# Output copies ahead of other VectorE work at block seams, a changed prologue order and two moved units, in a fused Fourier filter and SwiGLU kernel

## Chip, cores, metric

One core of one Trainium2 chip. The time is the device time of one execution, in microseconds (us), as a median over runs. The **span** in a profile is the time from the first to the last instruction of one profiled execution; it is some 2 us shorter than the run's time (890.6 in a run of 892.44 us). Every run lists its mean granted TensorE clock, where 1.0 is full speed.

## The reference

```python
X = np.fft.rfft(x, axis=1)                       # x: 8 sequences, 3008 tokens, 256 channels
y = np.fft.irfft(X * (filt_r + 1j * filt_i)[None], n=3008, axis=1)
x = y.reshape(24064, 256)
xn = x / np.sqrt(np.mean(x * x, axis=-1, keepdims=True) + 1e-6) * rms_g
g, val = xn @ w_gate, xn @ w_val                 # d_ff = 1536
out = (g * (1 / (1 + np.exp(-g))) * val) @ w_out
```

## The kernel before

The transforms are matmuls in two stages. "Stage A" transforms a sequence along one factor of its length. "Stage B" transforms along the other: a *unit* is a pair of matmuls into a bank (`psb`), followed by two products with the filter tables `fr` and `fi` and then by inverse matmuls. The feed-forward part runs over blocks of 512 tokens; each block takes 12 *slots* (one per 128 columns of d_ff, `JT = 12`). In a slot TensorE makes gate and value (`pg`, `pv`), ScalarE makes `sg`, VectorE multiplies them to `hh`, and two slots later `down` adds `hh` times `w_out` to the output banks `po0` and `po1`. Units of the *next* sequence are spread over the slots of the current one; only sequence 0 has nothing to hide behind, so it has a *prologue* of some 47 us, in which dummy matmuls (`warm_up`) keep TensorE active.

VectorE takes its work in the order of issue, so the loop that issues the slots sets the order:

```python
def at(slot, fn, *a):
    todo = {q_unit: late, swap_unit: pre}.get(fn, plan).setdefault(slot, [])
    ...
for i in range(len(items) + 4):
    for fn, a in pre.get(i, ()):      # half-swaps of summed units
        fn(*a)
    if i < len(items):
        gv(*items[i])                 # pg, pv, sg, hh
    for fn, a in plan.get(i, ()):     # stage A and B units, inverses, loads
        fn(*a)
    if 2 <= i < len(items) + 2:
        down(*items[i - 2])           # after a block's last slot: copies po0 (ScalarE), po1 (VectorE)
    for fn, a in late.get(i, ()):
        fn(*a)
```

A stage B unit of a later sequence, and the two ways in which VectorE can be spared (`summed`: one full product, two half-swaps, GpSimd adds; `eng = gpsimd`: ScalarE copies the bank, GpSimd makes both products):

```python
def b_unit(b, i, ps=None):
    ps = b_mm(b, i)                                   # bank "mb", one buffer, for b > 0
    f1, f2 = filt(2 * i, 2)
    ... # cut: the tiles s1 and s2
    if b and summed(b, i):
        nc.vector.tensor_tensor(out=s1, in0=ps, in1=f1, op=ALU.mult)      # L252
        return                                        # half-swaps L278, L276 follow in swap_unit
    eng = nc.vector
    if (i in (3, 5, 8, 12)) if b else (i in (3, 7, 9, 12)):
        eng = nc.gpsimd
        ... # cut: the tile v
        nc.scalar.activation(out=v, in_=ps, func=AXT.Copy)                # L266
        ps = v
    eng.tensor_tensor(out=s1, in0=ps, in1=f1, op=ALU.mult)                # L268
    eng.tensor_tensor(out=s2, in0=ps, in1=f2, op=ALU.mult)                # L269
```

The middle of the prologue, where ScalarE (`A`) copies filter tables to the other half of the partitions (`f_dup`), and `inverses` of the second unit of a pair ends with ScalarE's copy of the pair's banks to `gT` (L578; `pgt` is the bank):

```python
products(1); stage_b(5); t1_copy(5, 1)
... # cut
products(4, 7)                       # 7, 9 and 12 go to GpSimd
... # cut
products(5); inverses(3); stage_b(9); products(6, 9); stage_b(10, 11)
inverses(4); products(8); stage_b(12); inverses(5)
f_dup(3, 1, A, 0, 4)
products(12); ...; products(10); stage_b(13, 14); inverses(6)
f_dup(3, 1, A, 4, 8)
inverses(7); products(11); stage_b(15); inverses(8); products(13)
```

## Time and profile before

893.53 us, median of 3 runs (893.45 to 894.48).

| | before | how to read it |
|---|---|---|
| span of the profiled run | 890.6 us, clock 0.999 | undisturbed |
| first gate matmul (`pg<-xn`) starts | 47.15 us | end of the prologue |
| from there to the end | 843.4 us | 588 slots |
| busy share of TensorE, VectorE, ScalarE, GpSimd | 98, 77, 70, 49% | "busy" of TensorE includes the drain |

A matmul's bar in a timeline is longer than its share of the engine, so I use the distances between starts: what a start comes later than the normal distance (0.109 us after a 128x256 matmul, 0.216 after a 128x512, the median of its form after a smaller one) is a **hole**. Over the 843.4 us the holes of more than 0.03 us are 22 and sum to 8.4 us.

### The profile page before, as it was taken

The numbers are of one execution on the slowest core, as the hardware profiler recorded it, in microseconds if no ns is written. First come the engines' busy times: TensorE is split into PE (matmuls) and PEld (weight loads), VectorE is DVE, ScalarE is ACT, GpSimd is POOL, SyncE is SP. The second block draws the span as 40 slices with busy tenths as digits, with TensorE's granted clock in tenths as the row PEclk, the third lists the DMA queues.
The fourth block names the chain that finished last, engine by engine and source line by source line (L and its number), as shares of the span: only waits on it lengthen the run. The fifth ranks groups of instructions, "written<-read, shape, count | busy, mean of one in ns | idle before, by whom it ended". The sixth has DMA issues, their size and how long they took to land.

```text
span 890.6 us, 17468 instructions
## 1 busy us (share of the span) xinstructions
PE 873.5 (98%) x6258; PEld 559.4 (63%) x6258; DVE 681.5 (77%) x1091; ACT 625.1 (70%) x1068; POOL 435.6 (49%) x392
## 2 busy tenths in 40 slices
PE   8799999999999999999999999999999999999997
PEld 5666666666666666666666666666666666666556
DVE  7866787889987877888688787888878887555555
ACT  7877657677677766877677766787657765676444
POOL 7843830656427661677236662376515762155300
PEclk9999999999999999999999999999999999999999
DMA  8696726675663456335645247233352232222202
GB/s 196 122 196 156 157 67 207 143 158 110 162 159 89 101 111 185 107 90 113 159 119 132 86 81 199 80 94 90 88 163 72 67 90 61 85 66 49 72 24 48
DMA packets 80095, 101.44 MB, mean 114 GB/s; under 512 B 8108, under 2 KB 56684, under 8 KB 79560
## 3 DMA queue, kind: packets, MB, share of 16 engines
q1 hardware_dynamic: 69688, 84.23, 34.8%
q0 software_dynamic: 10240, 15.96, 11.4%
q8 instruction: 49, 0.80, 0.4%
q14 instruction: 38, 0.31, 0.1%
q10 hardware_dynamic: 80, 0.13, 0.1%
HBM read 67.67 MB, written 46.78 MB: 129 GB/s over the span
## 4 chain that ended last, share of the span: by engine, by line
PE 87%; issue 4%; DVE 2%; ACT 2%; DMA 2%; POOL 2%; SPq 0%; ACTq 0%; POOLq 0%; DVEq 0%
PE po L462 26%; PE pg L443 25%; PE pv L443 25%; PE psi L291 3%; PE psb L238 3%; PE psn L323 2%; PE psa L203 2%; DMA fr<-in_filt_r_dram 1%; DVE o L469 1%; ACT fr L516 1%; DVE hh L448 1%; DMA rb<-r_tmp 1%; ACT gT L578 1%; PE psq L352 0%; POOL xc L188 0%
## 5 line engine op out<-in xcount | busy, mean ns | idle before, releaser
L448 DVE TENSOR_TENSOR hh<-pv,sg 128x512 f16<-128x512 f32 (+2 forms) x588 | 392.9, 670 | 190.2 <-ACT sg L447 77.6
L447 ACT ACTIVATE sg<-pg 128x512 f16<-128x512 f32 (+2 forms) x588 | 340.9, 580 | 227.5 <-PE pg L443 217.8
L462 PE MATMUL po<-wo,hh 128*128 128x256 f16 x2244 | 343.2, 272 | 3.8 <-DVE o L469 3.0
L443 PE MATMUL pv<-xn,wv 128*128 128x512 f16 (+2 forms) x1176 | 339.6, 370 | 0.0
L443 PE MATMUL pg<-xn,wg 128*128 128x512 f16 (+2 forms) x1176 | 339.5, 370 | 0.0
L462 PEld LDWEIGHTS <-hh 128*128 128x128 f16 x2256 | 216.4, 98 | 99.0 <-issue 5.3
L282 POOL TENSOR_TENSOR s<-s,s 128x512 f16<-128x512 f16 x102 | 117.9, 1157 | 237.5 <-DVE s L276 165.6
L443 PEld LDWEIGHTS <-wv 128*128 128x128 f16 x1176 | 114.9, 98 | 128.8 <-issue 0.3
L419 POOL TENSOR_TENSOR xn<-y,rb 128x1024 f16<-128x1024 f32 (+1 forms) x45 | 126.0, 2801 | 44.9 <-DMA rb<-r_tmp 37.7
L443 PEld LDWEIGHTS <-wg 128*128 128x128 f16 x1176 | 111.4, 98 | 13.0 <-issue 0.3
L358 POOL TENSOR_TENSOR rho<-u,mhalf 128x4 f32<-128x4 f32 (+1 forms) x48 | 49.1, 1022 | 63.5 <-DVE u L356 63.1
L276 DVE TENSOR_TENSOR s<-psb,fi 64x512 f16<-64x512 f32 x102 | 69.8, 684 | 3.1
L296 ACT ACTIVATE t<-psi 96x512 f16<-96x512 f32 x112 | 66.4, 593 | 8.1 <-PE psi L291 2.7
L278 DVE SCALAR_TENSOR_TENSOR s<-psb,fi 64x512 f16<-64x512 f32 x102 | 70.7, 693 | 1.4
L252 DVE TENSOR_TENSOR s<-psb,fr 128x512 f16<-128x512 f32 x102 | 69.4, 681 | 0.0
L329 ACT ACTIVATE y<-psn,gsb 128x512 f32<-128x512 f32 (+1 forms) x94 | 63.8, 679 | 7.8 <-PE psn L323 0.5
L343 POOL TENSOR_TENSOR sq<-sq 128x512 f16<-128x512 f16 (+1 forms) x35 | 39.6, 1133 | 35.9 <-ACT sq L335 35.9
L335 ACT ACTIVATE sq<-psn 128x512 f16<-128x512 f32 (+1 forms) x94 | 54.8, 583 | 0.0
L208 ACT ACTIVATE t<-psa 128x512 f16<-128x512 f32 x70 | 41.8, 597 | 5.6 <-PE psa L203 2.4
L291 PE MATMUL psi<-s,wi 128*128 128x256 f16 x236 | 44.1, 273 | 0.0
L238 PE MATMUL psb<-t,wb 96*128 96x256 f16 x224 | 43.0, 272 | 0.5 <-DVE s L269 0.5
L323 PEld LDWEIGHTS <-t 128*128 128x128 f16 x368 | 28.4, 98 | 20.6 <-issue 0.4
(104 smaller groups left out, 523.1 us busy)
## 6 DMA issues: line engine op xcount, KB each, us to landing
out_dram<-o SPq DMA_DIRECT2D x83, 256.0 KB
xc<-in_x_dram POOLq DMA_DIRECT2D x56, 192.0 KB, 5.8
z_tmp<-t SPq DMA_DIRECT2D x28, 384.0 KB
t<-z_tmp SPq DMA_DIRECT2D x28, 384.0 KB
g_tmp<-t SPq DMA_DIRECT2D x56, 192.0 KB
rb<-r_tmp SPq DMA_DIRECT2D x41, 256.0 KB
t<-g_tmp SPq DMA_DIRECT2D x21, 384.0 KB
t<-g_tmp SPq DMA_DIRECT2D x7, 320.0 KB
```

The costliest lines, as they stand in the source:

```text
L238: nc.tensor.matmul(ps[:, u, :], w[:, k, :], t, start=True, stop=True)
L252: nc.vector.tensor_tensor(out=s1, in0=ps, in1=f1, op=ALU.mult)
L276: nc.vector.tensor_tensor(out=s2[a], in0=ps[e], in1=f2[e], op=ALU.mult)
L278: nc.vector.scalar_tensor_tensor(out=s2[a], in0=ps[e], scalar=-1.0, in1=f2[e], op0=ALU.mult, op1=ALU.mult)
L282: nc.gpsimd.tensor_tensor(out=s, in0=s1, in1=s2, op=ALU.add)
L291: nc.tensor.matmul(ps[:, u, :], wi_at(q, 2 * i + u), ss[q][:, u, :], start=(q == 0), stop=(q == n - 1))
L296: nc.scalar.activation(out=st[b]["t3"][c][:, 2 * r:2 * r + 2, :], in_=ps[0:KR], func=AXT.Copy)
L419: nc.gpsimd.tensor_tensor(out=xv, in0=yv, in1=rv.unsqueeze(1).to_broadcast([P, 2, n, P]), op=ALU.mult)
L443: nc.tensor.matmul(ps[:, 0:w], wt[:, dt_, ts(jt, P)], xn[:, dt_, :], start=(dt_ == 0), stop=(dt_ == 1))
L447: nc.scalar.activation(out=sg[:, 0:w], in_=pg[:, 0:w], func=AXT.Silu)
L448: nc.vector.tensor_tensor(out=hh[:, 0:w], in0=pv[:, 0:w], in1=sg[:, 0:w], op=ALU.mult)
L462: nc.tensor.matmul(po[s4 // per][:, s4 % per, :], hh[:, ts(s4, P)], wo[:, jt, :], start=(jt == 0 and s4 % per == 0), stop=(jt == JT - 1 an ...
```

## The change

The intent is to close isolated holes on TensorE. At a block's seam (slot 1 modulo 12) stage A and B units are issued after the output copies. Two units of sequence 1 are moved (15 to GpSimd, 1 a slot later), one q step of sequence 2 comes a slot later, and the prologue gets fewer dummy matmuls ("fillers"), one table build earlier and two copies on other engines.

```diff
-        return b > 1 or b == 1 and i in (6, 7, 10, 11, 14, 15)
+        return b > 1 or b == 1 and i in (6, 7, 10, 11, 14)
...
-        if (i in (3, 5, 8, 12)) if b else (i in (3, 7, 9, 12)):
+        if (i in (3, 5, 8, 12, 15)) if b else (i in (3, 7, 9, 12)):
...
             if m == 4:
-                warm_up(6, 0)
+                warm_up(5, 0)
...
-            for g in ((4, 5), (6,), (), (), (7,), ())[m]:
+            for g in ((4, 5), (6,), (), (7,), (), ())[m]:
                 wi_group(g)
             if m == 4:
-                warm_up(3, 0)
+                warm_up(1, 0)
...
-            t1_copy(g, g == 1)
+            t1_copy(g, g % 2)
...
+        t1_copy(4, 0)
         f_dup(0, 0, A, 0, 2)
...
-        t1_copy(4, 1)
         f_dup(0, 0, A, 4, 8)
...
-            todo = {q_unit: late, swap_unit: pre}.get(fn, plan).setdefault(slot, [])
+            at_seam = slot % JT == 1 and fn in (a_unit, b_unit)
+            todo = late if at_seam or fn == q_unit else pre if fn == swap_unit else plan
+            todo = todo.setdefault(slot, [])
...
-                r = (4, 8, 12)
+                r = (5 if (b, m) == (2, 1) else 4, 8, 12)
...
-                b_at = [22 + 7 * i // 4 for i in range(16)]
+                b_at = [22 + 7 * i // 4 + (i == 1) for i in range(16)]
```

## The prediction

> **What bounds the kernel now.** I read the page first (busy shares and the slices), then the table of windows, then the list of what TensorE waited for, then the timeline of VectorE and TensorE around each of those waits, and last the chain of waits over the first 50 us.
>
> ```profile
> PE 873.5 (98%) x6258; PEld 559.4 (63%) x6258; DVE 681.5 (77%) x1091; ACT 625.1 (70%) x1068; POOL 435.6 (49%) x392
> ...
> PE   8799999999999999999999999999999999999997
> ...
> 300.00:400.00 100.00, 100.00 (x699) 64.29 (x698) 80.88 (x129) 74.39 (x129) 55.73 (x50) 1.00 0.50 121
> ```
>
> TensorE is the bound, and in the middle it has nothing left to give: in 300 to 400 us it is busy for 100.00 of 100.00 us at full granted clock (1.00). What can be saved is idle time in the first 45 us, or isolated holes after that. The holes are few, and the list of TensorE's waits names most of them:
>
> ```profile
> PE po L462 <- DVE o L469: 3.0, 6, 0.8
> PE psb L238 <- DVE s L269: 0.5, 2, 0.3
> PE psq L352 <- POOL sq L343: 0.5, 1, 0.5
> ```
>
> "Busy" includes the drain of a pipelined matmul, so I size each hole from the distance between starts: a 128x256 matmul normally starts 0.109 us after the one before it, a 128x512 one 0.216 us (medians over this trace). The largest hole, in the timelines of VectorE and then TensorE:
>
> ```profile
> 109.06 0.69 DVE L448 TENSOR_TENSOR hh<-pv,sg 128x512 f16<-128x512 f32 x1 [0.92 <-PE psb L238]
> 109.66 0.68 DVE L268 TENSOR_TENSOR s<-psb,fr 128x512 f16<-128x512 f32 x1
> 110.26 0.68 DVE L269 TENSOR_TENSOR s<-psb,fi 128x512 f16<-128x512 f32 x1
> 110.86 0.68 DVE L469 COPY o<-po 128x512 f32<-128x512 f32 x1
> ...
> 110.40 0.38 PE L462 MATMUL po<-wo,hh 128*128 128x256 f16 x2
> 111.59 0.38 PE L462 MATMUL po<-wo,hh 128*128 128x256 f16 x2 [0.81 <-DVE o L469]
> ```
>
> A token block is 12 slots. The slot after its last one is a seam: the output bank `po1` is finished, VectorE must copy it out, and TensorE wants the bank again one slot later. Two stage B products (L268, L269) stand ahead of the copy. Third `po` matmul: 111.59 - 110.40 - 0.22 = **0.97 us** lost.
>
> **What the Trainium skill says.** "Perfetto Trace Analysis", section Identifying the Most-Contended Engine, says matmul busy share is no measure of headroom, as matmuls are pipelined; this trace agrees: at 98% busy there are holes of up to 0.97 us that the starts show. "TensorE: Matmul & The Clock Gate" gives in its opening table a strict first-in first-out queue for ScalarE, VectorE and GpSimdE. The trace agrees: the copy above was ready with `po` long before 110.86 and still ran third. So order of issue alone can open or close a hole. The same page, section What's actually happening, says the matmul clock halves after about 3.4 us of idleness; that is why dummy matmuls stand in the prologue. The largest TensorE wait in the first 50 us here is 1.2 us and the granted clock stays 1.00 in the windows, so dropping three of them should not cost clock.
>
> **The change part by part.**
>
> *1. Seams.* At a slot that is 1 modulo 12, stage A and B units go behind the output copies. By the slot formulas only five seams hold such a unit or the moved one: slots 13, 25, 37, 49, 61. From sequence 3 on, no unit falls on a seam, so the rest of the run does not move. Holes, from starts as above: slot 13 (70.4 us) 0.77 - 0.60 = 0.17; slot 25 90.31 - 89.33 - 0.22 = 0.76; slot 37 0.97; slot 61 150.87 - 150.19 - 0.22 = 0.46. In each the copy would start right behind `hh`. At slot 37 it would run 109.66 to 110.34, and TensorE wants the bank at 110.62: no wait. The products end when they ended before. Together 2.36 us.
>
> *2. Unit 15 of sequence 1 moves from VectorE to GpSimd.* Its two half-swaps, done at seam 49, are not reordered by part 1 (swaps stay ahead), so it is moved instead.
>
> ```profile
> 129.00 0.69 DVE L278 SCALAR_TENSOR_TENSOR s<-psb,fi 64x512 f16<-64x512 f32 x1
> 129.70 0.68 DVE L276 TENSOR_TENSOR s<-psb,fi 64x512 f16<-64x512 f32 x1
> 130.42 0.69 DVE L448 TENSOR_TENSOR hh<-pv,sg 128x512 f16<-128x512 f32 x1
> 131.03 0.68 DVE L469 COPY o<-po 128x512 f32<-128x512 f32 x1
> ```
>
> The hole there is 131.76 - 130.71 - 0.22 = 0.83 us and goes. The price: the unit is no longer summed before its inverse, so 4 matmuls of 128x256 in place of 2, 2 x 0.109 = 0.22 us on TensorE; ScalarE gets a copy of 0.6 us, GpSimd two products of 1.27 us for one add of 1.16 us. GpSimd is busy 17.5 of 50 us there, and the inverse comes four slots (over 5 us) later. Net gain 0.61 us.
>
> *3. Unit 1 of sequence 1 one slot later.* At 83.7 us the second stage B matmul waits for products of unit 0: 84.37 - 83.92 = 0.45 us, which goes. But unit 1 now sits one slot before unit 2. I place them by adding durations: unit 1's products end near 87.5 us, while unit 2's matmul (same bank) would be ready near 87.35, so about 0.2 us comes back. Net 0.25 us.
>
> *4. A later q step for block 1 of sequence 2.* TensorE waits for GpSimd's fold at 272.7: 273.35 - 272.70 = 0.65 us. One slot (1.3 us) later the fold, done at 273.3, is in time. The broadcast load stays where it was, with 3 slots in place of 4 after the q step; 0.65 us gained.
>
> *5. Prologue.* Three fillers of 0.216 us go: the first transposes of stage 1 start 0.65 us sooner. One copy of 1.02 us leaves ScalarE after the first filter piece and another comes before it. But the filter tables come by DMA, and the same ScalarE copies wait for those: the first may not start before 20.9 us, the second group not before 25.3 (it ran at 25.82). The last piece ends it all:
>
> ```profile
> 30.09 0.57 SPq L518 DMA_DIRECT2D fr<-fr  x1
> ...
> L268 DVEq EVENT_SEMAPHORE  x6: 21/35/2078, 30.5 to 36.1; - x6
> ...
> 34.78 0.69 DVE L268 TENSOR_TENSOR sg<-psb,fr 128x512 f16<-128x512 f32 x1 [0.38 <-PE pgt L570]
> ```
>
> VectorE's sequencer sat 2.08 us (32.56 to 34.64) in a semaphore wait; the trace's semaphore events show that the DMA issued at 30.09 finished at 34.61. The matmul named in the bracket is only the last event by the profile. From 34.78 VectorE runs without a pause to 38.46, the last product. Nothing in the change moves that DMA. ScalarE's chain beside it gains, after its own DMA waits (27.5 and 28.0 us), some 0.13 us. So I give the prologue **0.13 us**, not the 0.65 us or the 1.02 us that its edits suggest.
>
> Sum: 2.36 + 0.61 + 0.25 + 0.65 + 0.13 = 4.0 us. 893.53 - 4.0 = **889.5 us**.
>
> **The rivals.**
>
> *A. The prologue gives all it seems to.* If the DMAs are not the gate (the chain of waits puts most of 21 to 40 us on ScalarE, where I see its copies back to back), the shift of 0.65 us, perhaps up to 0.9, arrives at the end of the prologue. For it: ScalarE's row names no DMA wait after 21 us but was often ready just at a landing. Against it: the 2.08 us wait. It would make 888.7 to 889.0.
>
> *B. The delayed products take the copy's place as the wait.* With the copy first, products end up to 0.7 us later relative to `hh`, and the bank for stage B has a single buffer. If the next unit's matmul meets them, as in part 3, a hole moves instead of closing. At 37 and 61 the next user of the bank is two or more slots off; only slot 25 is tight. It would make 890 to 890.5.
>
> *C. Another engine becomes the bound.* VectorE at 40.3 of 50 us in 100 to 150 us is the nearest, but the change takes work from it. GpSimd: its `xn` products of 2.87 us could be delayed by unit 15 or by the later q step, and token blocks would start late; there are five slots (over 6 us) between `xn` and use. Above 891 if true; unlikely.
>
> **Range and chances.** The parts are read from visible holes and only parts 3 and 5 are estimates, worth some 0.5 us up or down each; the three runs of before spread over 1.0 us. All together: 888.3 to 891.1. A change of 2% is 17.9 us, more than all holes left after 45 us (about 10 us by starts), so within 2% is nearly certain.
>
> **What would show it right or wrong.** In TensorE's waits, the row for the output copy falls from 6 times, 3.0 us to 2 times (the swap seams near 165 and 240 us, which I expect to keep 0.57 and 0.43 us), and the row for the fold goes. Stage B waits: one near 97 us stays, and a short one of about 0.2 us appears near 87 us. VectorE's product of unit 13 still starts at about 34.7 us and the gate matmuls at 47.0 to 47.1 us; a start before 46.6 would say rival A. The span falls from 890.6 to about 886.6. I am wrong if a new wait of over 0.5 us on stage B's bank or on `xn` appears, or if the filter DMAs land at other times in other runs, which would shift the prologue either way.

## The result, and the profile after

**889.29 us** (888.32 to 890.67, 4 runs) against 893.56 us of the kernel before in the same rounds: ratio 0.9951, 95% interval 0.9934 to 0.9968, so within 2%. A ratio here is the mean time of one kernel's fast runs over that of the other's of the same rounds, so it is not quite the ratio of the medians quoted. The profiled run has a span of 886.7 us at clock 1.0.

TensorE's row of the 40 slices and the middle of the run (start and end of the stretch, its length, then busy us of TensorE, weight loads, VectorE, ScalarE and GpSimd, granted clock, DMA share and GB/s) in the profile after:

```profile
PE   8799999999999999999999999999999999999998
```

```profile
300.00:400.00 100.00, 100.00 (x693) 63.87 (x692) 81.04 (x129) 74.50 (x130) 55.09 (x48) 1.00 0.50 121
```

Nothing moved in the middle, as it could not. The list of TensorE's waits (total us, times, longest) has shrunk where it was meant to:

```profile
PE po L462 <- DVE o L469: 0.7, 2, 0.4
...
PE psb L238 <- DVE s L269: 0.2, 1, 0.2
```

The output copy is waited for twice in place of six times and the row for GpSimd's fold is gone. At the seam of slot 37, VectorE and then TensorE in the timeline after:

```profile
107.95 0.69 DVE L448 TENSOR_TENSOR hh<-pv,sg 128x512 f16<-128x512 f32 x1 [0.74 <-PE po L462]
108.56 0.68 DVE L469 COPY o<-po 128x512 f32<-128x512 f32 x1
109.15 0.68 DVE L268 TENSOR_TENSOR s<-psb,fr 128x512 f16<-128x512 f32 x1
109.75 0.68 DVE L269 TENSOR_TENSOR s<-psb,fi 128x512 f16<-128x512 f32 x1
```

```profile
109.29 0.60 PE L462 MATMUL po<-wo,hh 128*128 128x256 f16 x4
```

The copy runs second instead of fourth, and the four `po` matmuls are one group (x4) without a pause, where before they came as two and two with 0.97 us lost between. The two products pay for it: the second starts 1.80 us after `hh` where it was 1.20 before. They end at 110.43 us and the next matmul into their bank starts at 110.59, so nothing waits for them.

In numbers: from the first gate matmul to the end 839.5 us in place of 843.4, **3.9 us less**; the holes are 17 and sum to 4.3 us in place of 8.4. That is 4.1 us closed, less 0.22 us for two more inverse matmuls of unit 15. The gate matmul itself starts at 47.20 us in place of 47.15. So all of the gain is after the prologue, and the prologue gave nothing that these profiles show. (Their start of the gate matmul scatters: 46.97 to 47.66 us in four undisturbed profiles with the old prologue, this kernel before and three runs below.)

That left two questions for experiments: do the parts behind the prologue add up as counted, and why did the prologue not move although it has less work in it?

### The profile page after: what moved, and what is told of

Read it like the earlier page. It is cut to its first block, busy times and chain, and to the rows that moved or that the text cites. A ratio compares the mean times of both kernels' runs of the same rounds, so it can differ in the third digit from the quotient of the medians.

```text
span 886.7 us, 17463 instructions
## 1 busy us (share of the span) xinstructions
PE 873.2 (98%) x6257; PEld 559.0 (63%) x6257; DVE 678.7 (77%) x1088; ACT 625.3 (71%) x1069; POOL 436.5 (49%) x393
## 4 chain that ended last, share of the span: by engine, by line
PE 93%; DVE 1%; ACT 1%; issue 1%
PE po L462 27%; PE pg L443 27%; PE pv L443 27%; PE psi L291 3%; PE psb L238 3%; PE psn L323 2%; PE psa L203 2%; DVE o L469 1%; PE psq L352 1%; PE pt L589 0%; DVE hh L448 0%; ACT gT L578 0%; ACT fi L516 0%; PE psr L404 0%; PE pw L619 0%
```

## The experiments

Twelve kernels in three calls. In each call the kernel before ran in the same rounds: medians 893.59, 893.48 and 892.88 us. "Gate" is the start of the first gate matmul in the profiled run, and "rest" the time from there to the end. Splitting each span so keeps a disturbance of the prologue out of the verdict on the seams. In some kernels an added line shifts the line numbers by one (L269 for L268).

### Only the seams, only the prologue, only the units, and all with the old fillers

The seams alone (added to the kernel before):

```diff
+            at_seam = slot % JT == 1 and fn in (a_unit, b_unit)
+            todo = late if at_seam or fn == q_unit else pre if fn == swap_unit else plan
```

> The kernel before with the seam rule alone (stage A and B units behind the output copies). Theory: the holes at slots 13, 25, 37 and 61 close, 2.36 us; unit 1 is not moved here, so unit 2 has no neighbour and nothing comes back. Span 890.6 to about 888.2, ratio 0.997. TensorE waits for the output copy fall from 6 to 3 (the swap seams, 49 among them, stay). Rival (the delayed products take over as the wait): the waits for products in stage B grow by as much, and the span stays above 889.5.

890.80 us (889.89 to 891.71), ratio 0.9963 (0.9948 to 0.9979). Rest 841.33 us, 2.11 less. In its list of TensorE's waits:

```profile
PE po L462 <- DVE o L469: 1.3, 3, 0.7
```

Three waits stay: the two swap seams and slot 49, where the half-swaps of unit 15 are still ahead. The four holes of 2.36 us are gone; a new one of 0.30 us stands ahead of a stage A matmul that starts at 60.59 us. The span, 889.0 us, is above the 888.2 expected, because the gate matmul came at 47.66. No wait on stage B's bank appeared at 25, so the rival of delayed products falls for these units.

The prologue alone:

```diff
-                warm_up(6, 0)
+                warm_up(5, 0)
...
+            for g in ((4, 5), (6,), (), (7,), (), ())[m]:
...
-                warm_up(3, 0)
+                warm_up(1, 0)
...
-            t1_copy(g, g == 1)
+            t1_copy(g, g % 2)
...
+        t1_copy(4, 0)            # ahead of the f_dups, in place of t1_copy(4, 1) after them
```

> The kernel before with the prologue edits alone (three fillers out, one weight group earlier, two copies placed otherwise). As predicted (DMA gate): 0.13 us gained. Rival A: 0.65 us or more. New theory from the profile after: VectorE's unbroken row of copies and products from 21.6 to 31.85 us is the gate, its length is unchanged within 0.1 us, so the first gate matmul starts at 47.1 to 47.3 as before (47.15) and the span is 890.5 to 890.8 at full clock.

894.57 us (892.38 to 899.77), ratio 1.0017 (0.999 to 1.0043). Rest 843.43 us, as before. Its one run at clock 1.0 has a span of 890.5 us; the kernel before had 890.5 to 891.0 in its five runs at clock 1.0. So no gain is shown, and one of more than half a microsecond is unlikely. In the other five the mean clock was 0.991 to 0.998, and in the profiled one TensorE's clock was at half from 31.0 to 34.4 us. So these edits gave no time that shows, and more spread.

The two units and the q step alone (the first two, the `r` and the `b_at` lines of the diff):

> The kernel before with the three small moves alone (unit 15 to GpSimd, unit 1 a slot later, the q step of block 1 of sequence 2 a slot later). Theory: 0.61 + 0.45 + 0.65 us less what comes back of the second. Unit 2 keeps its place ahead of the down matmuls here, so unit 1's products must end before it: the wait that comes back is larger than in the full change, some 0.4 to 0.5 us, and the hole at slot 25 stays. Net 1.2 to 1.5 us, span near 889.2.

892.32 us (890.57 to 893.57), ratio 0.998 (0.9962 to 0.9998). Rest 841.74 us, 1.70 less: 0.61 from unit 15, 0.65 from the q step, and at seam 25, where the expectation had the hole stay, one of 0.20 in place of 0.76. But unit 1's move costs more here than it does beside the seams:

```profile
87.86 0.39 PE L238 MATMUL psb<-t,wb 96*128 96x256 f16 x2 [0.49 <-DVE s L269]
```

With 0.65 us lost there in place of the 0.45 that it removes, moving unit 1 pays through what it does to the seam, not at its own wait. Seams and units together: 2.11 + 1.70 = 3.81, and the whole change gained 3.91. That agreement is partly luck: both kernels close the hole at seam 25 (0.76 and 0.56 us, of which only 0.76 can count), while the hole of 0.30 at 60 us and 0.44 of the wait of unit 1 stand in the parts alone.

The changed kernel with the old fillers:

```diff
-                warm_up(5, 0)
+                warm_up(6, 0)
...
-            for g in ((4, 5), (6,), (), (7,), (), ())[m]:
+            for g in ((4, 5), (6,), (), (), (7,), ())[m]:
...
-                warm_up(1, 0)
+                warm_up(3, 0)
```

> The changed kernel with the fillers and the weight group of before. New theory: the first copies are 0.4 us later, so VectorE's row starts 0.3 to 0.5 us later and the gate matmuls with it: span 887.0 to 887.2 at full clock. If the DMA gates, nothing changes: 886.7. On the clock: the changed kernel showed a mean clock of 0.995 in two of its four runs, 2 us longer. If the missing fillers cause that, this kernel shows 0.999 or 1.0 in all runs; if it is chance, it shows 0.995 in some too, and so does the kernel before.

890.14 us (889.08 to 890.5), ratio 0.9955 (0.994 to 0.9969). Rest 839.53, the same as after. Its three runs at clock 1.0 have spans of 887.3 to 887.7, those of the changed kernel 886.5, 886.7, 886.8 and, in its later repeat, 887.7. So fewer fillers may be worth up to 0.9 us, but the two ranges touch and it is not shown. The profiled run shows half clock again, from 30.5 to 37.3 us, with the old fillers in place; so the new fillers are not needed for the fall.

### What the prologue waits for

The prediction held that the DMA of the last filter piece (`fr<-fr`) gates it: product 13 of VectorE waited for it until 34.78 us. After the change that DMA landed 1.6 us earlier (33.01 us in place of 34.61), product 13 did not wait at all, and VectorE's last product ended at 38.04 us in place of 38.46:

```profile
33.78 0.68 DVE L269 TENSOR_TENSOR hh<-psb,fi 128x512 f16<-128x512 f32 x1
34.37 0.68 DVE L268 TENSOR_TENSOR sg<-psb,fr 128x512 f16<-128x512 f32 x1
...
37.36 0.68 DVE L269 TENSOR_TENSOR hh<-psb,fi 128x512 f16<-128x512 f32 x1
```

Yet the gate matmul came at 47.20 us. So the landing did not set it there. ScalarE's timeline of the kernel before, then of the one after, shows where the two runs agree to 0.06 us:

```profile
32.02 0.60 ACT L266 ACTIVATE v<-psb 128x512 f32<-128x512 f32 x1
32.64 0.87 ACT L578 ACTIVATE gT<-pgt 128x384 f16<-128x384 f32 x2
33.54 1.06 ACT L516 ACTIVATE fi<-fi 64x1024 f32<-64x1024 f32 x1
...
35.92 0.85 ACT L578 ACTIVATE gT<-pgt 128x384 f16<-128x384 f32 x2
```

```profile
31.16 0.60 ACT L266 ACTIVATE v<-psb 128x512 f32<-128x512 f32 x1
32.70 0.87 ACT L578 ACTIVATE gT<-pgt 128x384 f16<-128x384 f32 x2 [0.93 <-PE pgt L570]
33.59 1.06 ACT L516 ACTIVATE fi<-fi 64x1024 f32<-64x1024 f32 x1
...
35.97 0.85 ACT L578 ACTIVATE gT<-pgt 128x384 f16<-128x384 f32 x2
```

After the change ScalarE arrives earlier and then stands idle for 0.93 us, until an inverse matmul (L570) is done, and from 32.70 on it is back to back as before. That inverse stands on TensorE behind the stage B matmul of unit 12, which needs the bank that VectorE's products of unit 8 free, and VectorE is without a longer pause from the first product of unit 4 (26.91 us before, 26.98 after) through unit 8. This gives a new theory: **VectorE's row of products from unit 4 to 8, then ScalarE's row of copies, set the end of the prologue, and the last filter DMA does not.** The view of the chain of waits had said as much before the change: it lies on ScalarE's pieces and the inverse matmuls from 20.99 to 40.38 us, and the DMA of 30.09 is not in it. Two runs test the theory from both sides.

The first takes the DMA away: products of units 12 to 15 read the filter piece before (the result is wrong, relative error 0.33).

```diff
-        f1, f2 = filt(2 * i, 2)
+        f1, f2 = filt(2 * i - (KC if b == 0 and i > 11 else 0), 2)
```

> The kernel before, with units 12 to 15 of sequence 0 multiplied by the filter chunk before (wrong numbers on purpose): nothing waits for the last filter DMA any more. As predicted (that DMA gates): VectorE's product of unit 13 starts some 0.4 us earlier and the first gate matmul moves from 47.15 to below 46.8. New theory (VectorE's row up to unit 8, then ScalarE's row from 32.6 us on is the gate): product 13 starts earlier, and the gate matmul stays at 47.1 to 47.5.

892.23 us in one run, span 890.3. VectorE and ScalarE in its timelines:

```profile
26.73 0.69 DVE L268 TENSOR_TENSOR ss<-psb,fr 128x512 f16<-128x512 f32 x1
...
34.15 0.68 DVE L268 TENSOR_TENSOR sg<-psb,fr 128x512 f16<-128x512 f32 x1
```

```profile
32.47 0.87 ACT L578 ACTIVATE gT<-pgt 128x384 f16<-128x384 f32 x2
```

Product 13 starts 0.63 us earlier than before, without a wait. The gate matmul starts at 46.97, 0.18 us earlier, and so did unit 4's first product (0.18) and the `gT` copy (0.17), which all lie ahead of the piece that was taken away. (The gate had been expected at 47.1 to 47.5 by the new theory and below 46.8 by the prediction's.)

The second lengthens the row: unit 8's first product is made twice (the result stays right).

```diff
-        eng.tensor_tensor(out=s1, in0=ps, in1=f1, op=ALU.mult)
+        for _ in range(2 if (b, i) == (0, 8) else 1):
+            eng.tensor_tensor(out=s1, in0=ps, in1=f1, op=ALU.mult)
```

> The kernel before with VectorE's first product of unit 8 done twice, 0.6 us more on its row. New theory: everything behind moves by the whole 0.6 us, ScalarE's gT copy of pair 2 from 32.64 to about 33.2 and the first gate matmul from 47.15 to 47.75 (more or less 0.3, as filter DMAs land differently). DMA gate: the wait of 0.38 us of product 13 absorbs most of it, at most 0.25 us later.

893.65 us in one run, span 891.8. Again VectorE, then ScalarE:

```profile
31.01 1.41 DVE L269 TENSOR_TENSOR ss<-psb,fr 128x512 f16<-128x512 f32 x2
```

```profile
33.87 0.87 ACT L579 ACTIVATE gT<-pgt 128x384 f16<-128x384 f32 x2 [0.74 <-PE pgt L571]
```

| kernel | unit 4's first product | `gT` copy of pair 2 | gate | unit 4 to gate |
|---|---|---|---|---|
| before | 26.91 | 32.64 | 47.15 | 20.24 |
| after | 26.98 | 32.70 | 47.20 | 20.22 |
| DMA taken away | 26.73 | 32.47 | 46.97 | 20.24 |
| product made twice | 27.41 | 33.87 | 48.38 | 20.96 |

The distance is constant to 0.02 us where the row has the same work. The product made twice put 0.72 us more on the row (unit 8's second product starts 1.32 us after its first in place of 0.60), and the distance grew by 0.73. The theory holds in both directions, though each of these runs is a single one, and the second's gate came later than expected (48.38 us, not 47.75): 0.50 us of that is unit 4's own later start.

What sets the start of the row was not tested. In the kernel before ScalarE's first filter copy waited 0.37 us for the *first* filter DMA, and in a run below it waited 1.73 us for it; unit 4 started at 26.73 to 27.43 us in the five profiles with the old order of copies and fillers and no dummies added.

The theory also suggests why the change gained nothing: its copy of group 4 (L557) moved from ScalarE to VectorE, ahead of that row, and that of group 3 went the other way. VectorE before, then after:

```profile
21.65 0.69 DVE L268 TENSOR_TENSOR ss<-psb,fr 128x512 f16<-128x512 f32 x1 [0.28 <-ACT fr L516]
...
24.30 0.69 DVE L268 TENSOR_TENSOR ss<-psb,fr 128x512 f16<-128x512 f32 x1 [0.17 <-ACT fr L516]
...
26.91 0.69 DVE L268 TENSOR_TENSOR ss<-psb,fr 128x512 f16<-128x512 f32 x1
```

```profile
21.59 0.69 DVE L557 COPY t<-pt 96x1024 f16<-96x1024 f16 x1 [1.22 <-PE pt L549]
22.20 0.68 DVE L268 TENSOR_TENSOR ss<-psb,fr 128x512 f16<-128x512 f32 x1
...
26.98 0.67 DVE L268 TENSOR_TENSOR ss<-psb,fr 128x512 f16<-128x512 f32 x1
```

VectorE waits 1.22 us for the transposes of group 4 and copies it for some 0.6 us ahead of the first product; in exchange the later waits for ScalarE go. The first product starts 0.55 us later and unit 4's 0.07 later: a wash. In the run with the old copies and the new fillers (below) unit 4 starts at 26.91 us, so the copies gained nothing there either.

### Why the clock falls in some runs

The profiled runs of the prologue alone and of the changed kernel with old fillers had half clock in one stretch that begins near 30 us, 3.4 us long in the first and 6.8 in the second. Is it the moved copies? The changed kernel with the old ones:

```diff
-            t1_copy(g, g % 2)
+            t1_copy(g, g == 1)
...
-        t1_copy(4, 0)
...
+        t1_copy(4, 1)
```

> The changed kernel with the three moved copies of the prologue back where they were (fillers still fewer). Clock: so far kernels with the old copies fell to a mean clock of 0.996 or less in 1 of 23 runs, those with the moved copies in 7 of 16. If the copies cause it (TensorE has longer pauses between 24 and 28 us), at most one run here does; if it is chance, two or three. Span at full clock: theory (VectorE's row of copies and products is the gate, and here one copy is off it but it waits for ScalarE) 886.4 to 887.0, as the changed kernel.

890.07 us (888.75 to 890.41), ratio 0.9963 (0.995 to 0.9976), and half clock from 30.1 to 36.9 us in the profile. Three of its five runs had a mean clock of 0.996 or less, so the copies alone are not the cause. Together with the run with old fillers this means that neither half of the prologue edits is needed for the fall.

Is it then too little work for TensorE? Two more dummy matmuls for each stage B unit up to 11:

```diff
-            nc.tensor.matmul(ps[:, 0, :], wz[:, 0:P], wz[:, 0:D], start=True, stop=True)
+            for _ in range(3 if i < 12 else 1):
+                nc.tensor.matmul(ps[:, 0, :], wz[:, 0:P], wz[:, 0:D], start=True, stop=True)
```

> The changed kernel with three dummy matmuls in place of one ahead of stage B of sequence 0's units 4 to 11: 16 more of 0.109 us, in TensorE's pauses from 23 to 31 us. If low TensorE load there lets the clock fall, no run here has a mean clock of 0.996 or less, and the runs lie within 1 us of each other; cost at full clock at most 0.3 us. If the clock does not depend on it, two or three of the runs are at 0.996 or less.

888.81 us (888.58 to 893.88), ratio 0.996 (0.9943 to 0.9978). Five of six runs were at 888.58 to 889.13 with clock 0.999 to 1.0. The sixth, which was also the profiled one, took 893.88 us: a weight table landed late, TensorE waited 1.33 us for it, and the clock was at half from 10.1 to 20.4 us, in a stretch without the added dummies. The same dummies in the kernel before, and the changed kernel once more as a control:

> The kernel before with the same 16 dummy matmuls added and nothing else. In the traces so far the clock fell to half at 30 to 31 us in the three runs whose TensorE load in the clock window that ended there was 0.28 to 0.32, and kept full clock at 0.35 and more. If so, this kernel shows no fall near 30 us, most runs have a mean clock of 0.999 or 1.0, and its time is some 0.5 us under the mean of the kernel before (892.7 to 893.2). If the clock does not depend on that load, clock and time are spread as those of the kernel before.

893.94 us (892.65 to 894.25), ratio 1.0002 (0.9969 to 1.0035); clock 0.999 to 1.0 in all five runs. Unit 4 to gate is 20.47 us, so the dummies cost 0.23 us. The clock was as expected, the time was not: the kernel before seldom loses the clock there, so it gains nothing from them.

> The changed kernel once more, to have more of its runs beside the others: about 889.3 us, a mean clock of 0.996 or less in one to three of the runs, span at full clock 886.5 to 886.9.

889.57 us (888.61 to 891.18), ratio 0.9956 (0.9926 to 0.9985). The gain of the change repeats. Two of the five runs had a low mean clock; the two at clock 1.0 had spans of 886.8 and, outside what was expected, 887.7 us. Its profiled run (889.97 us) fell to half clock from 30.1 to 36.9 us. Here is the stretch from 28 to 32 us in that run, and then in the undisturbed run of the same kernel (columns as above):

```profile
28.00:32.00 4.00, 2.54 (x20) 1.76 (x21) 3.94 (x7) 3.95 (x7) 3.92 (x3) 0.76 0.58 121
```

```profile
28.00:32.00 4.00, 2.63 (x29) 1.94 (x30) 3.87 (x8) 3.72 (x6) 3.92 (x3) 1.00 0.72 161
```

The last but two column is the granted clock. Its steps in the traces lie 3.41 us apart, or multiples of that. I summed the normal start distances of all matmuls, dummies included, in each such window. Where the clock fell at its end, they filled 0.36 of it (prologue alone and old fillers), 0.38 (old copies) and 0.40 (the repeat). The windows that ended between 28 and 33 us in the other profiles kept the clock and were filled to 0.45 or more. But no level can be read from this: a window of the kernel before that ended at 38.3 us was filled to 0.38 and kept it. The 0.28 to 0.32 and the 0.35 that the expectation above names do not come out of such a sum. Sums near them come out when the dummies are left out, and then the first kernel of the next section kept the clock after a window filled to 0.28. Every kernel without the added dummies dips to about 0.3 for windows that would end between 30.3 and 31.2 us, those with them to 0.44 or more, so it seems to depend on where the windows fall in a run. In these traces a fall near 30 us costs about 1.1 to 1.3 us: unit 4 to gate was 21.3 to 21.5 us in place of 20.2.

| kernels | runs | mean clock 0.996 or less |
|---|---|---|
| original prologue | 45 | 2 |
| any edited prologue | 26 | 12 |
| either, with the dummies | 21 | 1 |

So the change's prologue loses the clock more often, and low load in the window near 30 us goes with it. Which of its edits does that stays open: old copies or old fillers alone did not remove it. Where the clock fell in runs that were not profiled is not known; four of them (two of the kernel before, two of the prologue alone) took 897 to 900 us, more than a fall near 30 us explains.

### Further than the change: swaps behind the copies too, and another order on ScalarE

Two holes after the change, 0.57 and 0.42 us, are at seams where half-swaps stand ahead of the copy. The next kernel puts swaps behind the copies as well, moves unit 5 of sequence 1 by a slot (for a hole of 0.38 us near 96 us), and has the dummies:

```diff
-            at_seam = slot % JT == 1 and fn in (a_unit, b_unit)
+            at_seam = slot % JT == 1 and fn in (a_unit, b_unit, swap_unit)
...
-                b_at = [22 + 7 * i // 4 + (i == 1) for i in range(16)]
+                b_at = [22 + 7 * i // 4 + (i in (1, 5)) for i in range(16)]
```

> The changed kernel with the 16 dummies, with the half-swaps at a seam behind the output copies too, and unit 5 of sequence 1 a slot later. Theory: the holes at the two swap seams (0.57 and 0.42 us) and at unit 5 (0.38 us) close: 1.37 us, span 885.2 to 885.6 at full clock, and few runs below it. Rival: the delayed half-swap holds stage B's bank and makes a new wait, then 886.3 or more.

891.47 us (891.3 to 892.31), ratio 0.9977 (0.9948 to 1.0005). Slower than the change: the rest is 842.24 us, 2.7 more. Its list of TensorE's waits, then VectorE and TensorE at one of those seams:

```profile
PE psb L239 <- DVE s L277: 3.3, 5, 0.8
```

```profile
161.25 0.41 DVE L470 COPY o<-po 128x256 f32<-128x256 f32 x1
161.70 0.69 DVE L277 TENSOR_TENSOR s<-psb,fi 64x512 f16<-64x512 f32 x1
```

```profile
162.44 0.39 PE L239 MATMUL psb<-t,wb 96*128 96x256 f16 x2 [0.84 <-DVE s L277]
```

The half-swap is the last reader of stage B's only bank. Behind the copy it comes too late for the next unit, and five holes of 0.71 to 1.00 us stand in place of three that summed to 1.37. The words "not of swaps" in the change are right: that is where the rival of delayed products is true.

The last kernel adds to this one another order on ScalarE, the inverse of unit 7 (with its `gT` copy) ahead of the last filter copy:

```diff
         inverses(6)
-        f_dup(3, 1, A, 4, 8)
         inverses(7)
+        f_dup(3, 1, A, 4, 8)
```

> The kernel of the run before with one order changed in the prologue: ScalarE copies the gT of pair 3 before the last filter duplication, not behind it. Theory (ScalarE's row from 32.6 us on gates, not the DMA): gT of pair 3 comes 0.9 us earlier, VectorE's second product of unit 14 is late by some 0.7 us instead, and the first gate matmul is 0.2 to 0.6 us earlier: the distance from VectorE's product of unit 4 to the gate matmul, 20.22 to 20.24 us in all runs at full clock so far, falls to 19.6 to 20.0.

891.83 us (890.48 to 892.15), ratio 0.9975 (0.9945 to 1.0004). Unit 4 to gate is 19.68 us in place of 20.46 in the kernel above: 0.78 us less, from the order of two pieces on ScalarE alone. The `gT` copy of pair 3 in the kernel above, then in this one:

```profile
36.00 0.85 ACT L579 ACTIVATE gT<-pgt 128x384 f16<-128x384 f32 x2
```

```profile
36.47 0.84 ACT L579 ACTIVATE gT<-pgt 128x384 f16<-128x384 f32 x2
```

Counted from unit 4's first product (26.76 and 28.17 us), it starts at 8.30 us in place of 9.24. That confirms the second half of the theory, ScalarE's row. The gain is shown in this distance alone: the median did not fall. Unit 4 itself started late in the profiled run (28.17 us), because ScalarE's first filter copy had waited 1.73 us for the first filter DMA, and that hid the gain in the span. This order was not run on the changed kernel by itself; the dummies alone on it gave the lowest median, 888.81 us, but at full clock both kernels are the same (five runs of 888.58 to 889.13 with dummies; 888.32, 888.58, 888.61 and 889.57 without).

## Why the prediction was right, and which step of it was wrong

The time predicted was 889.5 us, and 889.29 came out; the range and "within 2%" held. That the median lies within 0.2 us is luck in part. It stands between two runs at clock 1.0 (888.32 and 888.58) and two at 0.995 (889.99 and 890.67), and the prediction had no loss of clock in it. The gain of the two undisturbed spans, 890.6 less 886.7, is 3.9 us against 4.0 predicted, and that is what the parts below account for.

- **Part 1, seams: right in size and mechanism.** All four holes are gone (2.36 us predicted). (Two slips of the text changed nothing. The copy before the change ran third behind `hh`, fourth of the lines shown. And the products do not "end when they ended before": beside `hh` they end 0.6 us later.) Done alone, the seams took 2.11 us off the rest, since a hole of 0.30 us appeared at 60 us in that kernel.
- **Part 2, unit 15: right.** The hole of 0.83 is gone and two matmuls more are there, net 0.61.
- **Part 3, unit 1: right beside the seams, with the return of 0.2 us as placed** (0.21 us ahead of the matmul at 87.44 us, too short for the list of waits), net 0.24 against 0.25. Alone, the unit's own wait would have grown to 0.65 us; the prediction did not see that its two parts lean on each other.
- **Part 4, the q step: right.** The row for the fold is gone, 0.65 us.
- **Sum of parts 1 to 4**: 3.87 us predicted, 3.91 measured from the gate matmul on.
- **Part 5, the prologue: the wrong step.** "The last piece ends it all", and "Nothing in the change moves that DMA". The landing moved by 1.6 us, product 13 started at 34.37 us and not at 34.7, and the prologue's end did not follow; with the DMA taken away it moved only as much as unit 4 had. The true gate is VectorE's row of products to unit 8 and ScalarE's row behind it. The predicted 0.13 us measured as -0.05, a difference that one pair of profiles cannot tell from none (scatter 0.7 us); the size was nearly right because both theories give little, and for the wrong reason. The 2.08 us that VectorE's sequencer sat in a wait was slack: VectorE itself, still at work on earlier products, was idle for 0.38 us of it. The chain of waits, which the prediction set aside under rival A, had ScalarE there and not this DMA.
- **The clock: a statement that was wrong.** "Dropping three of them should not cost clock" went by the longest single wait. The falls near 30 us came at the end of windows in which no idle stretch was longer than 1.01 us but matmuls filled only 0.36 to 0.40, and the edited prologues had a low mean clock in 12 of 26 runs against 2 of 45. That the edit of the fillers is what brings them is not shown.
- **Rivals.** A (the prologue gives 0.65 us or more) fell: the gate did not come before 46.6 us, and the prologue alone gave 1.0017. Its reading that ScalarE is the gate was right, though. B (a delayed product becomes the wait) is false for the units that the change moves, and true for swaps. C (another engine becomes the bound) did not show: no row of TensorE's waits for `xn` appeared. (VectorE was nearest the bound in 200 to 250 us, 45.03 of 50 us, and not in the stretch that C names.)

## What to carry to other kernels

When a finished bank must be drained by an in-order engine at a fixed moment, look at what stands ahead of the drain in that engine's order, and move only work whose own bank is not needed soon. To find a gate, do not take the longest wait: start from the chain of waits, take the distance from a candidate to the end in two runs, and accept it only if the distance stays the same when something else moves; then lengthen it by a known amount. An edit can make the clock fall in some of the runs, which a single undisturbed profile will not show: compare the clock of every run.

## What the Trainium skill lacked or had wrong

- "TensorE: Matmul & The Clock Gate", section What's actually happening, gives one idle window of about 3.4 us as the condition for the half clock. The free-running window of 3.41 us agrees with the traces. But here the clock fell after windows that were not idle: matmuls filled 0.36 to 0.40 of them. The same page, section A second HAM failure mode: psum-queue depth-cycling, has frequent short idle times between groups of matmuls make the clock swing. It gives no level at which that begins; here none came out either, as one window filled to 0.38 kept the clock.
- No page that I used says that the clock can fall in some runs of one kernel, and not in others, after it has once been at full speed; here 12 of 26 runs of kernels with an edited prologue had a mean clock of 0.996 or less, and a fall near 30 us cost about 1.1 to 1.3 us.
- "Perfetto Trace Analysis", section Optimization Strategy (under Identifying Performance Opportunities), has the reader find what blocks a gap on the engine in question. It lacks that a long wait, here 2.08 us of VectorE's sequencer (0.38 us of it idle time of the engine), can be slack: with it gone, the end of the prologue moved by 0.18 us, all of which lay ahead of it.
